# Nine neighbouring rows of w_mod on a partition, and c loaded to match

## The chip, the cores and the metric

The kernel runs on one core of one Trainium2 chip. The metric is the device time of one execution in microseconds (us); the lower the better. Engines are named as in the profile: PE is TensorE (PEld its weight loads), DVE is VectorE, ACT is ScalarE, POOL is GpSimd, SP is SyncE, which only issues DMAs here.

## What is computed

A diffusion-transformer block with adaptive layer norm, in bf16. Two samples (B = 2) of N = 256 tokens with D = 1152 features:

```python
def reference(x, c, wqkv, wo, w_mod):
    B, N, D = x.shape
    mod = (_silu(c) @ w_mod).reshape(B, 6, 1, D)
    shift_a, scale_a, gate_a, shift_m, scale_m, gate_m = [mod[:, i] for i in range(6)]
    h = _layernorm(x, axis=-1) * (1 + scale_a) + shift_a
    qkv = h @ wqkv
    q, k, v = (qkv[..., :D].copy(), qkv[..., D:2 * D].copy(), qkv[..., 2 * D:].copy())
    p = _softmax(jnp.einsum('bqd,bkd->bqk', q, k) * D ** (-0.5), axis=-1)
    a = jnp.einsum('bqk,bkd->bqd', p, v) @ wo
    return x + gate_a * a
```

`w_mod` has 1152 rows of 6 x 1152 columns; only the first three sixths of the columns (shift, scale, gate) are used. `c` has one row of 1152 features for each sample. The product `silu(c) @ w_mod` sums over the 1152 features, and the sum may be taken in any order, as long as feature i of c meets row i of w_mod.

## The kernel before

**Tiles.** A feature dimension of 1152 is cut into KT = 9 blocks of P = 128 partitions, the 512 tokens (T) into TT = 4 tiles of 128. `x_sb` holds the tokens on partitions; `xn` is x normalized; `xnT` is xn transposed (features on partitions), made by nine PE transposes into `tp` for each token tile, and copied out by ACT or DVE. `hTs` is xnT times (1 + scale); the K projection is made from hTs alone, as a shift of h adds the same to all scores of one query. `hT` has scale and shift and feeds Q and V.

**c and the modulation.** c is loaded at line 118 on ACT's DMA queue as `c_sb`, 18 partitions (sample and block) of 128 features. PE transposes it at line 157 into `cT_ps` in PSUM, so that a partition holds the features p, p + 128, p + 256 and so on of both samples. `e_sb` is exp(-c) by ACT (line 166). `silu_c` (line 170) makes the silu on DVE: add one, reciprocal, times c, into `scT_f` (128 partitions x 9 x 2); ACT then copies it, repeated 27 times along the columns, to `scT_rep` in bf16. `sc_rhs(kk)` is block kk of it, the moving operand of the modulation's matmuls.

`wmod_v` (line 49) is the view of w_mod in which partition p and block kk mean row kk * 128 + p. `load_mod` issues loads from it on SP: `wS` (scale), `wH` (shift) and `wG` (gate, in the buffer of wS). `scale_A(kk)` multiplies block kk of wS with sc_rhs(kk), four matmuls of 54 columns, into `psS0` and `psSA`; `scale_B` and `shift_block` do the same for the other columns and for the shift. The gate is made on DVE: 18 `gate_step`s multiply a block of wG by the column of scT_f for that block and add it to `gacc`, and POOL sums gacc over the partitions to `gate_bc`, whose end is multiplied into `wo_last`.

**Fillers.** Behind the transpose of c, PE runs eight matmuls of 512 columns on `ident` and `junk_rhs` into `junk_ps`; their result isn't used. `ident` is made on POOL (lines 99 and 100), `junk_rhs` on DVE (line 105).

**Order.** The wrapper `_Rec` (line 65) records every instruction of PE, DVE, ACT and SP; `pin` fixes each engine's order to the order of the program text. So most instructions have line 74, the wrapper's call, in the profile. On DVE the statistics of x tile 1 come first, then the silu of c, then the statistics of x tile 0, the normalization of tile 1 and of tile 0. On PE: the transpose of c, the fillers, one matmul each that presets psSA and psS0 with ones, scale_A(0) and (1), the transposes of tile 1, scale_A(2) and (3), the transposes of tile 0, scale_A(4) to (8), then the K projection. SP issues x tiles 1, 0 and 3, five loads of wS, then pieces of wK with x tile 2 between them, the rest of wS, wK and wH, and later wqv, wG and wO. The last wait of the start is that of `scaled(0, ...)`, the first hTs, which needs psS0 and xnT of tiles 0 and 1.

## Time and profile before

| | us |
|---|---|
| median of 3 runs | 102.11 (101.9 to 102.24) |
| the profiled execution | 101.58 |
| its span, first to last instruction | 99.6 |
| PE busy in the span | 91.3 |
| DVE, ACT, POOL busy | 67.2, 29.3, 28.5 |
| DMA | 21.04 MB, mean 211 GB/s |

The page cuts the span into 40 slices of 2.5 us; each digit is a busy share in tenths:

```profile
PE   0979899899999999999999999999999999999930
PEld 0318788874466444444458756656678656656620
DVE  1595885462165999999973999922148578798930
ACT  5057513520060872332240563221146200000000
POOL 5033312000000000000000000079999700599940
...
DMA  2999999999999999999997000000000002020321
```

PE and the DMA engines start together; the loads keep the DMA engines full until about 55 us, and PE is busy until the end. POOL's work at 65 to 79 us is the sum of the gate over the partitions, and at 86 to 96 us the product into wo_last. In a line of the timeline the columns are start, duration, engine, source line, operation, what is written from what, shapes, count, and in brackets how long the engine had idled and what ended that.

### The profile page before, as it was taken

The numbers are of one execution on the slowest core, as the hardware profiler recorded it, in microseconds if no ns is written. First come the engines' busy times: TensorE is split into PE (matmuls) and PEld (weight loads), VectorE is DVE, ScalarE is ACT, GpSimd is POOL, SyncE is SP. The second block draws the span as 40 slices with busy tenths as digits, with TensorE's granted clock in tenths as the row PEclk, the third lists the DMA queues.
The fourth block names the chain that finished last, engine by engine and source line by source line (L and its number), as shares of the span: only waits on it lengthen the run. The fifth ranks groups of instructions, "written<-read, shape, count | busy, mean of one in ns | idle before, by whom it ended". The sixth has DMA issues, their size and how long they took to land.

```text
span 99.6 us, 1801 instructions
## 1 busy us (share of the span) xinstructions
PE 91.3 (92%) x733; PEld 56.9 (57%) x733; DVE 67.2 (67%) x129; ACT 29.3 (29%) x58; POOL 28.5 (29%) x29
## 2 busy tenths in 40 slices
PE   0979899899999999999999999999999999999930
PEld 0318788874466444444458756656678656656620
DVE  1595885462165999999973999922148578798930
ACT  5057513520060872332240563221146200000000
POOL 5033312000000000000000000079999700599940
PEclk9999999999999999999999999999999999999999
DMA  2999999999999999999997000000000002020321
GB/s 61 296 284 382 400 391 389 384 405 403 381 388 390 393 405 374 372 371 375 409 408 282 22 0 0 0 0 0 0 0 10 0 0 87 31 84 34 118 79 40
DMA packets 16338, 21.04 MB, mean 211 GB/s; under 512 B 1355, under 2 KB 10827, under 8 KB 16331
## 3 DMA queue, kind: packets, MB, share of 16 engines
q1 hardware_dynamic: 16160, 20.93, 58.4%
q8 instruction: 5, 0.08, 0.3%
q10 hardware_dynamic: 171, 0.02, 0.1%
q14 instruction: 2, 0.02, 0.0%
HBM read 19.76 MB, written 1.18 MB: 210 GB/s over the span
## 4 chain that ended last, share of the span: by engine, by line
issue 51%; POOL 23%; DMA 10%; POOLq 8%; DVE 3%; SPq 1%; PE 1%; ACT 0%
POOL gate_bc L549 14%; POOL wo_last L570 9%; POOLq L649 8%; DMA x_sb<-in_x_dram 5%; DMA wK<-in_wqkv_dram 5%; DVE stats L74 1%; SPq L74 1%; PE ps L74 1%; POOL rstd L198 1%; DVE xn L74 0%; DVE hTs L74 0%; DVE mv_all L74 0%; POOL rstd L197 0%; ACT o_sb L74 0%; POOLq L570 0%
## 5 line engine op out<-in xcount | busy, mean ns | idle before, releaser
L549 POOL PARTITION_ALL_REDUCE gate_bc<-gacc x2 | 13.7, 6886 | 49.9 <-DVE gacc L74 49.9
L74 DVE SCALAR_TENSOR_TENSOR gacc<-wG,scT_f,gacc 128x1152 f32<-128x1152 bf16 x16 | 22.7, 1418 | 0.5
L74 PE MATMUL ps<-wqv,hT 128*128 128x384 bf16 x108 | 17.9, 327 | 0.0
L74 PE MATMUL ps<-hT,wqv 128*128 128x512 bf16 x81 | 17.6, 380 | 0.0
L74 PE MATMUL ps<-wO,attnT 128*128 128x384 bf16 x99 | 16.3, 327 | 0.0
L74 PEld LDWEIGHTS <-attnT 128*128 128x128 bf16 x117 | 10.9, 98 | 6.9 <-issue 0.2
L74 PEld LDWEIGHTS <-hT 128*128 128x128 bf16 x108 | 10.5, 98 | 6.7
L74 PEld LDWEIGHTS <-wK 128*128 128x128 bf16 x137 | 11.1, 97 | 5.8 <-issue 0.5
L74 PEld LDWEIGHTS <-wqv 128*128 128x128 bf16 x81 | 7.8, 97 | 9.6 <-DVE hT L74 0.4
L74 PE MATMUL acc<-hTs,wK 128*128 128x128 bf16 (+2 forms) x102 | 12.9, 279 | 0.4 <-DVE hTs L74 0.4
L570 POOL TENSOR_TENSOR wo_last<-wO,gate_bc 128x384 bf16<-128x384 bf16 x9 | 10.0, 1142 | 6.8 <-issue 6.8
L74 ACT CAST qkT<-ps 128x512 bf16<-128x512 f32 x10 | 5.8, 583 | 10.9 <-PE ps L74 10.9
L74 DVE TENSOR_TENSOR o_sb<-ga,x_sb 128x384 bf16<-128x384 f32 x11 | 7.9, 718 | 0.4
L74 DVE TENSOR_TENSOR ga<-ps,gate_bc 128x384 f32<-128x384 f32 x11 | 6.1, 554 | 2.8 <-PE ps L74 2.8
L74 ACT CAST v_sb<-ps 128x384 bf16<-128x384 f32 x10 | 4.8, 478 | 9.6 <-PE ps L74 9.6
L74 DVE BATCH_NORM_STATS2 stats<-x_sb 128x6 f32<-128x384 bf16 x9 | 4.5, 545 | 2.2 <-DMA x_sb<-in_x_dram 2.2
L74 ACT CAST o_sb<-ps 128x64 bf16<-128x64 f32 x1 | 0.2, 212 | 18.5 <-PE ps L74 18.5
L74 DVE CAST v_sb<-ps 128x384 bf16<-128x384 f32 x2 | 1.1, 557 | 6.0 <-PE ps L74 6.0
L74 DVE CAST attnT<-ps 128x512 bf16<-128x512 f32 (+1 forms) x6 | 3.5, 603 | 1.8 <-PE ps L74 1.8
L74 DVE CAST qkT<-acc 128x512 bf16<-128x512 f32 x3 | 1.9, 684 | 4.1 <-PE acc L74 4.1
L74 DVE TENSOR_SCALAR hTs<-xnT,s1p 128x256 bf16<-128x256 bf16 (+1 forms) x21 | 4.2, 270 | 0.6 <-ACT xnT L74 0.5
L74 PE MATMUL ps<-hTs,wK 128*128 128x512 bf16 x19 | 4.6, 378 | 0.0
(76 smaller groups left out, 88.2 us busy)
## 6 DMA issues: line engine op xcount, KB each, us to landing
wqv<-in_wqkv_dram SPq DMA_DIRECT2D x5, 864.0 KB, 10.7
wG<-in_w_mod_dram SPq DMA_DIRECT2D x3, 864.0 KB, 9.7
wO<-in_wo_dram SPq DMA_DIRECT2D x3, 864.0 KB, 8.6
wH<-in_w_mod_dram SPq DMA_DIRECT2D x4, 576.0 KB, 10.4
x_sb<-in_x_dram SPq DMA_DIRECT2D x4, 288.0 KB, 3.1
wS<-in_w_mod_dram SPq DMA_DIRECT2D x4, 256.0 KB, 5.6
wK<-in_wqkv_dram SPq DMA_DIRECT2D x4, 256.0 KB, 5.1
wK<-in_wqkv_dram SPq DMA_DIRECT2D x1, 864.0 KB, 11.0
```

The costliest lines, as they stand in the source:

```text
L74: r = fn(*a, **k)
L198: nc.gpsimd.tensor_tensor(out=rstd[:, t : t + 1], in0=rstd[:, t : t + 1], in1=neg_half, op=ALU.pow)
L549: ar = nc.gpsimd.partition_all_reduce(gate_bc[:, b, :], gacc[:, b, :], P, bass.bass_isa.ReduceOp.add)
L570: nc.gpsimd.tensor_tensor(out=wo_last[:, k, :], in0=wO[:, k, D - TAILW :], in1=gate_bc[:, B - 1, D - TAILW :], op=ALU.mult)
L649: with _tile.TileContext(nc) as tc:
```

## The change

Row p * 9 + kk of w_mod now goes to partition p, block kk, and c is loaded so that partition p holds features 9p to 9p + 8 of both samples. c then comes in the layout in which the silu is wanted, 128 partitions x 2 x 9, and is read from SBUF; the transpose and its PSUM tile are gone. The order of the instructions that remain is as before. The slices of columns that are loaded, and the number of loads, stay.

```diff
-    wmod_v = w_mod.rearrange("(kk p) (s n) -> p kk s n", p=P, s=6)
+    wmod_v = w_mod.rearrange("(p kk) (s n) -> p kk s n", p=P, s=6)
...
-    c_sb = const.tile([2 * KT, P], BF16)
+    c_sb = const.tile([P, B, KT], BF16)
     x_sb = act.tile([P, TT, D], BF16)
     nc.scalar.preload_act_table_set("natural_log_exp_and_others")
-    nc.scalar.dma_start(out=c_sb, in_=c.rearrange("b (k p) -> (b k) p", p=P))
+    nc.scalar.dma_start(out=c_sb, in_=c.rearrange("b (p k) -> p b k", p=P))
...
-    cT_ps = psum_b.tile([P, 2 * KT], BF16, tag="pb")
-    ten.transpose(cT_ps, c_sb, ident[: 2 * KT, : 2 * KT])
+    cT = c_sb.rearrange("p b k -> p (b k)")
     junk_ps = psum_a.tile([P, 512], F32, tag="pa")
...
     fillers(8)
     e_sb = small.tile([P, 2 * KT], F32, tag="e_sb")
-    sca.activation(out=e_sb, in_=cT_ps, func=ACT.Exp, scale=-1.0)
+    sca.activation(out=e_sb, in_=cT, func=ACT.Exp, scale=-1.0)
...
         vec.tensor_tensor(
             out=scT_f.rearrange("p k b -> p b k"),
-            in0=cT_ps.rearrange("p (b k) -> p b k", b=B),
+            in0=c_sb,
             in1=e_sb.rearrange("p (b k) -> p b k", b=B),
             op=ALU.mult,
         )
```

## The prediction

> **What bounds the kernel now.** I read the page's busy shares first, then the chain of waits from its end, then the waits, then the first 14 us in order of time, then the DMA queues of the first 4 us. PE is the engine with work nearly everywhere:

> ```profile
> PE 91.3 (92%) x733; PEld 56.9 (57%) x733; DVE 67.2 (67%) x129; ACT 29.3 (29%) x58; POOL 28.5 (29%) x29
> ```

> The end is released by a POOL chain, and that chain is released by VectorE, which has itself waited for PE. Chain of waits, then the list of waits:

> ```profile
> 65.43 13.69 POOL gate_bc L549 x2
> ...
> 86.94 8.92 POOL wo_last L570 x8
> ...
> 95.90 0.60 PE ps L74 x11
> ```

> ```profile
> POOL gate_bc L549 <- DVE gacc L74: 49.9, 1, 49.9
> ...
> DVE mx L74 <- PE s_ps L74: 2.0, 1, 2.0
> ...
> PE ps L74 <- POOL wo_last L570: 0.9, 1, 0.9
> ```

> The row maximum `mx` runs at 53.8 us and had to wait 2.0 us for the scores of PE; the gate steps, the all-reduce and `wo_last` follow it without a break. PE is busy in every microsecond from 20 to 53 (5.00 of 5.00 us in each stretch), so the scores come when the first 20 us let them. So whatever the change does to the start, late or early, moves the end by the same amount: a later start has nothing to hide in after 21 us, and an earlier one is good for up to the 2.0 us that `mx` waits. All of the change lies in the start. In order of time (start, duration, engine, work, and in brackets the idle time before it):

> ```profile
> 2.72 0.19 PE L74 MATMUL cT_ps<-ident,c_sb 18*128 18x18 bf16 x1 [2.72 <-DMA c_sb<-in_c_dram]
> 2.84 3.59 PE L74 MATMUL junk_ps<-junk_rhs,ident 128*128 128x512 bf16 x8
> ...
> 3.59 1.48 DVE L74 BATCH_NORM_STATS2 stats<-x_sb 128x6 f32<-128x384 bf16 x3 [2.21 <-DMA x_sb<-in_x_dram]
> ...
> 5.26 0.11 DVE L74 TENSOR_SCALAR e_sb<-e_sb 128x18 f32<-128x18 f32 x1
> ...
> 5.71 0.18 DVE L74 TENSOR_TENSOR scT_f<-cT_ps,e_sb 128x18 f32<-128x18 bf16 x1
> ...
> 7.46 0.23 PE L74 MATMUL psS<-scT_rep,wS 128*128 128x54 bf16 x1 [0.61 <-DMA wS<-in_w_mod_dram]
> ...
> 8.24 1.14 PE L74 MATMUL tp<-ident,xn 128*128 128x128 bf16 x9 [0.24 <-DVE xn L74]
> ...
> 9.56 1.14 PE L74 MATMUL tp<-ident,xn 128*128 128x128 bf16 x9
> ...
> 11.29 0.29 DVE L74 TENSOR_SCALAR hTs<-xnT,psS 128x256 bf16<-128x256 bf16 x1
> ```

> The path runs: first x load (lands just before 3.59), VectorE without a gap to xn(1) at 7.60 to 8.18, PE's transposes at 8.24, the two scale steps, the transposes of 9.56, the copies of xnT, hTs at 11.29, and PE's projection from 11.63 on. The PE waits at 7.46 (for wS) are not on it: PE would only wait for xn at 8.24 instead.

> **What is removed.** One weight load of 0.10 us and one matmul of 0.19 us, and with them PE's wait for c. PE idled there anyway, so by themselves they save nothing. But they stood ahead of the eight fillers. Now the fillers need only `junk_rhs` (VectorE, done at 0.90 + 0.48 = 1.38) and `ident` (POOL, 1.35 + 0.29 = 1.64). They start at about 1.70 in place of 2.84, 1.14 us sooner, and end at 5.29 in place of 6.43. The two small opening matmuls (to 6.85 now) follow, and then PE waits for wS until 7.46: some 1.75 us idle in place of 0.61. That wait costs nothing unless PE's clock minds it (below).

> **What is changed in VectorE and ScalarE.** The product `scT_f` reads c from SBUF and not from PSUM. It took 178 ns; the nearest 18-column rows that read SBUF alone are 114 ns (add) and 267 ns (reciprocal). So between -0.06 and +0.09 us, on the path, since VectorE has no gap from 3.59 to 7.55. It is nearer the 114 ns row, having no reciprocal, but has two tensor inputs: I take -0.03. The exponential (186 ns from PSUM; the 128x1 `nmean` row from SBUF 203 ns) has cover: ScalarE then waits 2.8 us.

> **What is added: c in 256 runs of 18 bytes.** Before, c came as 18 runs of 256 bytes on the ScalarE queue; now each of 128 partitions takes two runs of nine bf16, 16 runs for each of the 16 DMA engines. DMA queues of the first 4 us (packets, MB, share of 16 engines' time):

> ```profile
> q1 hardware_dynamic: 312, 0.65, 55.2%
> q10 hardware_dynamic: 27, 0.00, 0.6%
> ```

> q10 is c's queue: 0.6% of 16 x 4 us is 0.38 us, by 27 packets 14 ns each. q1 is the x loads: 55.2% is 35.3 us, by 312 packets 113 ns each. Price of c's 16 runs on each engine: from below 16 x 14 = 0.22 us, less the at most 0.04 us (two runs and an end mark) that it took before, 0.18 us; from above, if a tiny run costs as much as a row of x, 16 x 113 = 1.8 us. The nearer row in size and queue is the 14 ns, so 0.18. x goes to all 128 partitions through the same engines at the same time, eight rows on each, so at least half of c's runs go in before the first x load is done: 0.1 to 0.18 us late, and I count 0.17, a little above the middle since a run of 18 bytes may well cost somewhat over 14 ns. It is on the path (VectorE waits 2.21 us for just this load), so it counts in full: xn(1) later, transposes later, hTs later, all else as before.

> [...]

> Does c itself come late? If its runs alternate with x's, 16 x (14 + 113) = 2.0 us after x begins, that is about 4.1 in place of 2.7. The exponential (0.19) must be done by 5.26, when VectorE adds one: cover of 0.9 us is left. If it were gone, the first statistics of x(0), queued behind it on VectorE, would be late by as much.

> **w_mod's order.** The number and size of pieces stay (slices of 512, 640 or 1152 columns, one row a piece), and so do the issues and their order on SP's queue, and c's on ScalarE's; only which rows go to a partition changes. Loads of 864 KB take 9.7 us for w_mod (rows 13.8 KB apart), 10.7 for wqkv (6.9 KB) and 8.6 for wo (2.3 KB): no order by distance. Their spread, 10%, is the bound: of wS's 5.6 us to landing, 0.56 either way. Sooner saves nothing (PE then waits for xn). Later by 0.56 puts the first two scale steps at 8.02; their eight matmuls, 0.045 us apart, end the issue at 8.38, so the transposes come 0.15 us later. The wait of 0.61 is the cover, and I take 0. Sum: 0.17 - 0.03 = +0.14 us. Silu, scale, shift and gate pair the same feature of c with the same row of w_mod as before.

> The profiled execution is a span of 99.6 us and 2.0 us around it, 101.58 in all; the change makes it 101.72. The median of the runs is 0.53 above it, so 102.25.

> **Rivals.** *The clock opens later (slower).* The page's clock row reads 9 from the start, but the eight 512-column fillers take 3.59 us, 0.45 each, while later 81 of that shape take 17.64 us, 0.218 each: PE starts at half pace. In the rows the pace changes at 10.69 (four scale matmuls per 0.20 us before, per 0.10 after). Busy time of PE in four equal stretches that end there or after:

> ```profile
> 0.44:3.86 3.42, 1.14 (x4) 1.00 0.63 183
> 3.86:7.27 3.41, 2.93 (x9) 1.00 0.94 267
> 7.27:10.68 3.41, 2.98 (x38) 1.00 1.05 381
> ```

> If the change of pace needs a stretch this densely filled, the stretch to 7.27 loses over a microsecond of fillers and the one to 10.68 loses the delay of x. Then full pace comes a stretch later, say 3.2 us (7.46 to 10.69), at 13.9. The 16 scale matmuls left go at 0.05 in place of 0.025, +0.4 us; from 12.0 to 13.9 the 256-column matmuls go at 0.218 in place of 0.109 (six take 0.82), +0.95; PE's wait of 0.30 at 17.8 gives some back. About +1.05 with the 0.14 above, +1.2: 103.3. For it: the fillers are most of what PE does before 7.4. Against it: all 3.59 us of them changed nothing within 4 us here, so they may not matter at all. [...]

> *The clock opens sooner (faster).* If the pace follows the fillers' start, or the earlier fillers meet such a stretch better, PE is at full pace before 8.24. Then the first nine transposes take half, the second nine start with xn(0) (8.82 + 0.58 = 9.40) and end their first four by 9.84; the two copies (0.43 and 0.49) end at 10.83, and hTs starts at 10.88 in place of 11.29: -0.41, and wK's first piece, issued at 4.63 with 5.1 us to landing (the median of its kind), is there. 102.11 - 0.41 = 101.7; a later x load would take back 0.14.

> *Dear runs (slower).* If each 18-byte run costs like a row, the eight ahead of x's rows put the first load 8 x 113 = 0.9 us late: 103.0, at the utmost 1.8: 103.9. It decides from about 35 ns a run (8 x 35 = 0.3 us). Against it: 14 ns at 256 bytes.

> **Chances.** A measurement here tells 0.3% (0.31 us) from no change. The forecast, +0.14, own range 102.0 to 102.5: 0.40, of it 0.13 slower by more than that (c's runs at 30 ns or so) and 0.02 faster. Clock later 0.25, all slower. Dear runs 0.10, all slower. Clock sooner 0.25, 0.22 of it faster and 0.03 within. Slower 0.48, within 0.28, faster 0.24. The range runs from a little under the faster rival to the slower one, 101.6 to 103.3, and leaves out the upper end of the two slow ones and the lower end of the fast one, under 0.2.

> **What will show it.** The fillers at 1.7 and some 1.7 us of PE idle ahead of psS at 7.5; q10 with 256 more packets, less 18, of about 14 ns; the first statistics at 3.7 to 3.8 in place of 3.59; hTs as much later than 11.29; and the same distance at `mx` and at the end. A pace change far from 10.7 shows one of the clock rivals; a first x load over 0.4 us late shows dear runs; psS waiting for wS beyond 8.0 shows that w_mod's order matters. I am wrong if hTs moves without the first x load or the pace having moved.

## The result and the profile after

The changed kernel takes 103.49 us in the median (102.95 to 104.8) where the kernel before takes 102.11; the ratio is 1.0123, 95% interval 1.0082 to 1.0163. (Ratios here and below leave out the executions that ran over 1.5% above the fastest of their kernel, so a ratio need not be the quotient of two medians.) A second set of runs, with the experiments below, gave 1.0164 (1.0112 to 1.0217). So the change costs some 1.2 to 1.6%, against a forecast of +0.14 us. The time lies just above the range, which ended at 103.3.

The profiled execution took 103.77 us, with a span of 102.0 in place of 99.6. The start in order of time, the changed kernel:

```profile
1.70 3.59 PE L74 MATMUL junk_ps<-junk_rhs,ident 128*128 128x512 bf16 x8 [1.70 <-POOL ident L100]
...
3.49 1.48 DVE L74 BATCH_NORM_STATS2 stats<-x_sb 128x6 f32<-128x384 bf16 x3 [2.11 <-DMA x_sb<-in_x_dram]
3.67 0.22 ACT L74 ACTIVATE e_sb<-c_sb 128x18 f32<-128x18 bf16 x1 [1.67 <-DMA c_sb<-in_c_dram]
...
5.16 0.11 DVE L74 TENSOR_SCALAR e_sb<-e_sb 128x18 f32<-128x18 f32 x1
...
5.61 0.18 DVE L74 TENSOR_TENSOR scT_f<-c_sb,e_sb 128x18 f32<-128x18 bf16 x1
...
6.86 0.23 PE L74 MATMUL psS<-scT_rep,wS 128*128 128x54 bf16 x1 [1.16 <-DMA wS<-in_w_mod_dram]
...
8.33 0.16 DVE L74 SCALAR_TENSOR_TENSOR nb<-mv_all,rstd 128x1 f32<-128x1 f32 x1 [0.88 <-POOL rstd L197]
8.53 0.58 DVE L74 TENSOR_SCALAR xn<-x_sb,rstd,nb 128x1152 bf16<-128x1152 bf16 x1
9.16 1.14 PE L74 MATMUL tp<-ident,xn 128*128 128x128 bf16 x9 [1.76 <-DVE xn L74]
...
12.49 0.29 DVE L74 TENSOR_SCALAR hTs<-xnT,psS 128x256 bf16<-128x256 bf16 x1 [0.33 <-PE psS L74]
```

Nothing is late up to 7 us: the first statistics run at 3.49 (3.59 before), c and its exponential are there well before 5.16, and even the first wS comes sooner. Then VectorE stands for 0.88 us in front of the first `nb`, waiting for POOL, and with it xn(1) and the first transposes come 0.92 us late (9.16 against 8.24). POOL alone, in the kernel before and then in the changed one:

```profile
5.44 0.26 POOL L197 TENSOR_SCALAR rstd<-mv_all 128x1 f32<-128x1 f32 x1 [3.29 <-DVE e_sb L74]
...
5.79 0.60 POOL L198 TENSOR_TENSOR rstd<-rstd,neg_half 128x1 f32<-128x1 f32 x1
...
7.64 0.21 POOL L197 TENSOR_SCALAR rstd<-mv_all 128x1 f32<-128x1 f32 x1 [1.25 <-DVE nb L74]
```

```profile
5.34 0.26 POOL L196 TENSOR_SCALAR rstd<-mv_all 128x1 f32<-128x1 f32 x1 [3.20 <-DVE e_sb L74]
7.53 0.21 POOL L196 TENSOR_SCALAR rstd<-mv_all 128x1 f32<-128x1 f32 x1 [1.93 <-DVE mv_all L74]
7.70 1.44 POOL L197 TENSOR_TENSOR rstd<-rstd,neg_half 128x1 f32<-128x1 f32 x2
```

The two steps of rstd are an addition and a power. Before, POOL ran addition and power for tile 1, then both for tile 0. Now it runs both additions first, and the addition for tile 0 has to wait for tile 0's statistics until 7.53; the power for tile 1, ready since 5.6, stands behind it. POOL is the one engine whose order the kernel doesn't write out by hand: `pin` is called for PE, DVE, ACT and SP. The planner, given a program in which the silu takes c straight from a load, put POOL's instructions in another order. The diff shows nothing of it; a comparison of the two programs' POOL instructions does.

How the distance grows along the profiled execution (start in us):

| | before | after | distance |
|---|---|---|---|
| first nb | 7.46 | 8.33 | 0.87 |
| first transposes | 8.24 | 9.16 | 0.92 |
| first hTs | 11.29 | 12.49 | 1.20 |
| row maximum mx | 53.81 | 55.49 | 1.68 |
| sum of the gate on POOL | 65.43 | 67.11 | 1.68 |
| first wo_last | 85.87 | 88.35 | 2.48 |

From the transposes to mx it grows by 0.76. That fits PE at half pace for longer: a scale step of four matmuls takes 0.18 us up to the last one at 12.17, where the kernel before takes 0.10 from 10.69 on. The profile's record of the granted clock begins with its first change, here to full clock, at 13.83 in place of 10.68. The projection starts at 12.84, so its first 1.0 us runs at half pace and costs half of that, about the 0.48 from hTs to mx. From 67 to 88 us it grows by another 0.80, POOL's pause ahead of wo_last, 7.55 us in place of 6.75. In the profiles of the variants below that pause lies anywhere from 6.75 to 7.62 without any edit to that work (7.49 with w_mod's order alone), so I take this last step for a variation of one execution.

### The profile page after: what moved, and what is told of

It is laid out like the page before. It is cut to its first block, busy times and chain, and to the rows that moved or that the text cites. A ratio compares the mean times of both kernels' runs of the same rounds, so it can differ in the third digit from the quotient of the medians.

```text
span 102.0 us, 1800 instructions
## 1 busy us (share of the span) xinstructions
PE 92.0 (90%) x732; PEld 57.4 (56%) x732; DVE 67.9 (67%) x129; ACT 29.3 (29%) x58; POOL 28.4 (28%) x29
## 4 chain that ended last, share of the span: by engine, by line
issue 50%; POOL 24%; POOLq 8%; DVE 8%; PE 4%; DMA 3%; ACT 0%; DVEq 0%
POOL gate_bc L548 13%; POOL wo_last L569 9%; POOLq L648 8%; DVE stats L74 4%; DMA x_sb<-in_x_dram 3%; PE tp L74 2%; POOL rstd L197 1%; DVE xn L74 1%; DVE hTs L74 1%; PE psSA L74 1%; DVE mv_all L74 1%; PE ps L74 1%; POOL rstd L196 0%; PE psS L74 0%; DVE e_sb L74 0%
## 5 line engine op out<-in xcount | busy, mean ns | idle before, releaser
L74 DVE SCALAR_TENSOR_TENSOR gacc<-wG,scT_f,gacc 128x1152 f32<-128x1152 bf16 x16 | 22.7, 1418 | 0.5
L74 PE MATMUL ps<-wqv,hT 128*128 128x384 bf16 x108 | 17.9, 326 | 0.0
L74 PE MATMUL ps<-hT,wqv 128*128 128x512 bf16 x81 | 17.6, 379 | 0.0
L74 PE MATMUL ps<-wO,attnT 128*128 128x384 bf16 x99 | 16.3, 326 | 0.0
L74 PEld LDWEIGHTS <-attnT 128*128 128x128 bf16 x117 | 10.9, 98 | 7.5 <-issue 0.8
L74 PEld LDWEIGHTS <-wK 128*128 128x128 bf16 x137 | 11.3, 99 | 6.0 <-issue 0.4
L74 PEld LDWEIGHTS <-hT 128*128 128x128 bf16 x108 | 10.5, 98 | 6.7
L74 PE MATMUL acc<-hTs,wK 128*128 128x128 bf16 (+2 forms) x102 | 13.4, 285 | 0.3 <-DVE hTs L74 0.3
L74 PEld LDWEIGHTS <-wqv 128*128 128x128 bf16 x81 | 7.9, 98 | 9.6 <-DVE hT L74 0.4
L74 ACT CAST qkT<-ps 128x512 bf16<-128x512 f32 x10 | 5.8, 582 | 10.9 <-PE ps L74 10.9
L74 DVE TENSOR_TENSOR o_sb<-ga,x_sb 128x384 bf16<-128x384 f32 x11 | 8.3, 751 | 0.4
L74 DVE TENSOR_TENSOR ga<-ps,gate_bc 128x384 f32<-128x384 f32 x11 | 6.1, 555 | 3.0 <-PE ps L74 2.8
L74 ACT CAST v_sb<-ps 128x384 bf16<-128x384 f32 x10 | 4.8, 478 | 9.6 <-PE ps L74 9.6
L74 DVE BATCH_NORM_STATS2 stats<-x_sb 128x6 f32<-128x384 bf16 x9 | 4.5, 549 | 2.1 <-DMA x_sb<-in_x_dram 2.1
L74 PE MATMUL tp<-ident,xn 128*128 128x128 bf16 x36 | 3.9, 265 | 2.1 <-DVE xn L74 1.8
L74 ACT CAST o_sb<-ps 128x64 bf16<-128x64 f32 x1 | 0.2, 212 | 19.1 <-PE ps L74 19.1
L74 PE MATMUL junk_ps<-junk_rhs,ident 128*128 128x512 bf16 x8 | 3.6, 630 | 1.7 <-POOL ident L100 1.7
L74 DVE CAST v_sb<-ps 128x384 bf16<-128x384 f32 x2 | 1.1, 558 | 6.0 <-PE ps L74 6.0
L74 ACT COPY xnT<-tp 128x640 bf16<-128x640 bf16 (+1 forms) x5 | 3.2, 650 | 6.5 <-PE tp L74 6.5
L74 DVE TENSOR_SCALAR hTs<-xnT,s1p 128x256 bf16<-128x256 bf16 (+1 forms) x21 | 4.2, 272 | 1.1 <-ACT xnT L74 1.0
## 6 DMA issues: line engine op xcount, KB each, us to landing
wqv<-in_wqkv_dram SPq DMA_DIRECT2D x5, 864.0 KB, 11.5
wG<-in_w_mod_dram SPq DMA_DIRECT2D x3, 864.0 KB, 10.7
wH<-in_w_mod_dram SPq DMA_DIRECT2D x4, 576.0 KB, 10.7
```

Source lines behind the costliest of these rows:

```text
L74: r = fn(*a, **k)
```

## Experiments

"POOL held" below means that POOL's operations on rstd and nb are recorded and pinned, in the order of the program text, which is the order of the kernel before:

```diff
+    gps = _Rec(nc.gpsimd, pool_seq)
...
-        nc.gpsimd.tensor_scalar_add(out=rstd[:, t : t + 1], in0=mv_all[:, t, 1:2], scalar1=EPS)
-        nc.gpsimd.tensor_tensor(out=rstd[:, t : t + 1], in0=rstd[:, t : t + 1], in1=neg_half, op=ALU.pow)
+        gps.tensor_scalar_add(out=rstd[:, t : t + 1], in0=mv_all[:, t, 1:2], scalar1=EPS)
+        gps.tensor_tensor(out=rstd[:, t : t + 1], in0=rstd[:, t : t + 1], in1=neg_half, op=ALU.pow)
...
+    pin(pool_seq)
```

Every ratio is to the kernel before, run beside it on the same chip; the rows come from more than one chip.

| variant | POOL's order | fillers | ratio (95%) |
|---|---|---|---|
| changed kernel | new | 8, from 1.7 us | 1.0123 (1.0082 to 1.0163) |
| the same, again | new | 8, from 1.7 | 1.0164 (1.0112 to 1.0217) |
| changed, POOL held | old | 8, from 1.7 | 1.0068 (1.0025 to 1.0112) |
| the same, again | old | 8, from 1.7 | 1.0051 (0.9997 to 1.0105) |
| changed, fillers late | new | 8, from 3.4 | 1.0096 (1.0059 to 1.0134) |
| changed, POOL held, fillers late | old | 8, from 3.4 | 0.9958 (0.9910 to 1.0005) |
| changed, POOL held, 12 fillers | old | 12, from 1.7 | 0.9948 (0.9907 to 0.9989) |
| before, new POOL order | new | 8, behind c | 1.0124 (1.0089 to 1.0158) |
| before, fillers early | old | 8, from 1.7 | 1.0054 (1.0018 to 1.0091) |
| before, early, 12 fillers | old | 12, from 1.7 | 0.9959 (0.9919 to 0.9999) |
| before, 10 fillers | old | 10, behind c | 0.9958 (0.9920 to 0.9997) |
| before, w_mod's order alone | old | 8, behind c | 0.9988 (0.9953 to 1.0022) |

**The changed kernel with POOL held.**

> Theory P (POOL's order): in the changed kernel POOL computes both additions of rstd (tiles 1 and 0) before the first power, so nb(1) on VectorE waits for the second addition; 8.33 in place of 7.46 us. With POOL held to the old order, nb(1) comes at about 7.4, the first transposes at about 8.1 to 8.3 in place of 9.16, hTs at 11.2 to 11.5 in place of 12.49, and the time falls back to 101.9 to 102.5 us, within 0.4% of the kernel before. Rival C (clock, by the earlier fillers and the longer gap): the transposes come sooner too, but the pace still changes a stretch later than 10.7, and the time stays at 102.8 to 103.3 us. Rival D (c's small runs): the first x load is late and the time stays above 102.6.

102.45 us. VectorE's line, to be set beside the 8.33 above:

```profile
7.51 0.10 DVE L74 SCALAR_TENSOR_TENSOR nb<-mv_all,rstd 128x1 f32<-128x1 f32 x1
```

The wait is gone, the transposes start at 8.29. But hTs still came late, behind the scale matmuls (psS) at half pace, 0.18 us a step:

```profile
11.61 0.29 DVE L74 TENSOR_SCALAR hTs<-xnT,psS 128x256 bf16<-128x256 bf16 x1 [0.33 <-PE psS L74]
```

The time is 0.68% over the kernel before: POOL's order explains about half, and something is left. Run again:

> The changed kernel with POOL's order held, once more, on the same chip as the three others: C 102.3 to 102.8 us, 0.3 to 1.0% over the kernel before, the pace change in the trace at 10.5 to 14 us.

1.0051, with an interval that just touches one.

**The kernel before with POOL's new order.** The powers of tiles 1 and 0 are both issued after the addition for tile 0:

```diff
         gps.tensor_scalar_add(out=rstd[:, t : t + 1], in0=mv_all[:, t, 1:2], scalar1=EPS)
-        gps.tensor_tensor(out=rstd[:, t : t + 1], in0=rstd[:, t : t + 1], in1=neg_half, op=ALU.pow)
+        for u in {1: (), 0: (1, 0), 2: (2,)}[t]:
+            gps.tensor_tensor(out=rstd[:, u : u + 1], in0=rstd[:, u : u + 1], in1=neg_half, op=ALU.pow)
```

> The kernel before, with nothing changed but POOL's order: additions of rstd for tiles 1 and 0, then both powers. Theory P: nb(1) at 8.4 to 8.5 in place of 7.46, the first transposes at about 9.25 in place of 8.24, hTs 0.9 to 1.2 us later, 103.0 to 103.6 us. Rivals C and D: the fillers and c's load are as before, so the time stays at 101.9 to 102.4 us, save for at most 0.2.

103.17 us, 1.0124: POOL's order alone, with c, w_mod and the fillers untouched, costs about as much as the whole change. The same two lines in its profile:

```profile
7.77 1.44 POOL L74 TENSOR_TENSOR rstd<-rstd,neg_half 128x1 f32<-128x1 f32 x2
```

```profile
8.41 0.16 DVE L74 SCALAR_TENSOR_TENSOR nb<-mv_all,rstd 128x1 f32<-128x1 f32 x1 [0.88 <-POOL rstd L74]
```

The 0.88 us are not all of it. In this execution, the longest of the six at 104.11 us, PE stands idle for 1.35 us ahead of the transposes (0.24 before), the clock record begins only at 15.23, and mx comes at 56.20, 2.39 us later than before. So in this execution PE also stayed at half pace for longer, though nothing was done to the fillers: the stretch of 3.41 us in which PE waits for xn, from 8.40, is 2.58 us busy, where the kernel before had 2.98 from 7.27 and full pace behind it.

**w_mod's order alone.** Only line 49 is changed in the kernel before; c keeps its layout, so features of c meet other rows of w_mod: the output is another one, the work is the same.

> The kernel before with the new order of w_mod's rows alone; c is loaded and transposed as before, so features of c meet other rows of w_mod and the output is another one; the work is the same. Theory P: POOL's order is the old one here, and the time is that of the kernel before, 101.9 to 102.4 us. If w_mod's order matters to the loads: the wait for the first wS is 0.3 us or more longer or shorter and the time moves by over 0.3 us.

101.88 us, 0.9988: no cost shows. The 256 KB loads of wS take 5.5 us to landing (5.6 before), the 864 KB loads of wG 9.7 (9.7). With this, what is left of the loss must come from c's load or from the fillers.

**The kernel before with the fillers early.**

```diff
-    ten.transpose(cT_ps, c_sb, ident[: 2 * KT, : 2 * KT])
...
-    fillers(8)
+    fillers(3)
+    ten.transpose(cT_ps, c_sb, ident[: 2 * KT, : 2 * KT])
+    fillers(5)
```

> The kernel before with POOL's order held as it was, and the transpose of c put behind the third of the eight fillers, so that the fillers run from 1.7 to about 5.4 us in place of 2.84 to 6.43. c, w_mod and all loads are as before. If the earlier fillers and the longer gap after them are what is left of the loss with POOL's order held (C): the pace of PE changes later on average, hTs comes at up to 11.8, and the time is 102.5 to 102.9 us. If it is c's small runs or w_mod's order: the time stays at 101.8 to 102.3.

102.52 us, 1.0054. With c's old load, moving the same eight fillers 1.1 us ahead costs about as much as is left in the changed kernel with POOL held (1.0068 and 1.0051), and hTs is as late and waits for the same:

```profile
11.64 0.29 DVE L74 TENSOR_SCALAR hTs<-xnT,psS 128x256 bf16<-128x256 bf16 x1 [0.34 <-PE psS L74]
```

**The changed kernel with POOL held and the fillers late.**

```diff
-    vec.memset(junk_rhs, 1.0)
+    for _ in range(4):
+        vec.memset(junk_rhs, 1.0)
```

> The changed kernel with POOL's order held, and junk_rhs filled four times in place of once, so that the eight fillers start at about 2.8 us, as in the kernel before. C: the time falls from 102.5 to 101.8 to 102.3 us. If c's small runs or w_mod's order cost the rest: it stays at 102.4 to 102.9.

101.81 us, 0.9958. The fillers started later than meant, at 3.42, since each fill of junk_rhs begins 0.17 us after the end of the one before; so they end just before wS. With c's small runs and w_mod's new order in place, the loss is gone; whether there is a gain is open, as the interval reaches 1.0005. Its PE, to be set beside the 1.14 us for nine transposes:

```profile
3.42 3.57 PE L74 MATMUL junk_ps<-junk_rhs,ident 128*128 128x512 bf16 x8 [3.42 <-DVE junk_rhs L74]
...
8.37 0.68 PE L74 MATMUL tp<-ident,xn 128*128 128x128 bf16 x9 [0.74 <-DVE xn L74]
```

PE is at full pace at 8.37, and hTs comes at 10.80.

**The changed kernel with the fillers late and POOL's new order.**

> The changed kernel with POOL's order left as it is (both additions first) and junk_rhs filled four times, so that the fillers start at about 3.4 us and end near 6.9. If the two causes are separate, this keeps POOL's share alone: nb(1) at 8.3 to 8.4, the first transposes at 9.2, and 0.9 to 1.2 us more than the same kernel with POOL's order held (101.8): 102.6 to 103.0. If the whole loss were the clock's: 101.7 to 102.1.

103.28 us, 1.0096; against the same kernel with POOL held (0.9958) the order is 1.4% in the new layout, as it was 1.2% in the old. The ten executions lie between 101.58 and 104.25, so this ratio is looser than its interval says. The profiled one is the fastest of them and not typical: the other nine took 102.85 or more. In it the clock opened at 7.26 and stayed open, and PE waits for the late xn at full pace:

```profile
9.30 0.68 PE L74 MATMUL tp<-ident,xn 128*128 128x128 bf16 x9 [1.60 <-DVE xn L74]
```

VectorE still waits 0.88 us for POOL, but hTs comes at 11.36, only 0.56 us behind the variant with POOL held, and mx at 53.91, 0.59 us behind it and 0.10 us behind the kernel before. What the other nine did is not shown. So there are two causes, each of which costs by itself, but they don't simply add up: alone they give 1.0124 and 1.0054, together 1.0123 and 1.0164. In the profiles POOL's order costs more where PE is at half pace (2.39 us at mx above) than where it is not (0.59).

**The changed kernel again.**

> The changed kernel once more on the same chip as the other two: 102.9 to 103.8 us, 0.8 to 1.6% over the kernel before.

103.88 us, 1.0164. This execution shows the clock itself. Its stretches of 3.41 us, PE alone (stretch, length, PE busy and count, granted clock, DMA share, GB/s):

```profile
5.49:8.90 3.41, 0.55 (x10) 1.00 1.03 336
8.90:12.32 3.42, 3.03 (x43) 0.50 1.04 396
12.32:15.73 3.41, 3.04 (x36) 1.00 1.07 366
```

Here full pace came at 5.49, behind the early fillers (the first scale matmuls, at 6.59 and 6.71, are 0.12 us apart, against 0.19 in the profiled execution), but PE then worked only 0.55 us of the next 3.41, and behind that the granted clock was 0.50 for just the stretch in which the transposes run (9.29 to 11.5). In the profiled execution of the changed kernel the stretches lay otherwise:

```profile
3.59:7.01 3.42, 2.20 (x10) 1.00 0.94 304
7.01:10.42 3.41, 1.65 (x24) 1.00 1.05 378
10.42:13.83 3.41, 3.10 (x40) 1.00 1.06 379
```

The clock column reads 1.00 there only because the record begins at 13.83; the pace of the rows is half until then (1.14 us for nine transposes, against 0.68 with the fillers late). So in one of these two executions the early fillers were followed by half pace until 13.83, and in the other by full pace at 5.49 that was gone again at 8.90.

**Fillers without a gap.** Three variants fill PE up to the first scale matmul: the changed kernel with POOL held and `fillers(12)`, the kernel before with 3 fillers, the transpose and 9 more, and the kernel before with `fillers(10)`, all with POOL held.

> The changed kernel with POOL's order held and 12 fillers in place of 8, so that PE works without a gap from 1.7 to about 6.8 us and then takes the scale matmuls. Theory P alone: as with 8 fillers, 101.9 to 102.5 us, hTs at 11.2 to 11.5. If the pace of PE is set by how densely it worked before (C): the pace changes before 8 us, the nine transposes of a tile take about 0.7 us in place of 1.14, hTs comes at 10.8 to 11.0 and the time is 101.4 to 101.9 us.

> The kernel before with POOL's order held, c transposed behind the third filler and 12 fillers in all, from 1.7 to about 7.1 us. If the dense work from 1.7 us on is what made 12 fillers fast in the changed kernel (C), then it does as much here: 101.2 to 101.9 us, pace changed before 8 us in most executions. If the new layout itself gave that gain: 102.0 to 102.4.

> The kernel before with POOL's order held as it was and 10 fillers in place of 8, from 2.84 to 7.3 us, so that no gap is left before the scale matmuls. C: the pace changes before 8 us in most executions, 101.3 to 101.9 us. If the density before 7.4 does not matter: 102.0 to 102.3.

0.9948, 0.9959 and 0.9958. In the last, where c landed sooner and the fillers begin at 2.29 and not at 2.84, PE's fillers and transposes:

```profile
2.29 4.45 PE L74 MATMUL junk_ps<-junk_rhs,ident 128*128 128x512 bf16 x10
...
8.28 0.68 PE L74 MATMUL tp<-ident,xn 128*128 128x128 bf16 x9 [0.91 <-DVE xn L74]
```

By these ratios all three are faster than the kernel before, by a little and in either layout, so no gain of the new layout's own shows. It is a near thing: the intervals end at 0.9989, 0.9999 and 0.9997, and the median of all twelve executions of the first is 102.11 us, not the 101.4 to 101.9 expected and no less than that of the kernel before. Which is the best isn't settled. The simplest is two more fillers in the kernel before. (Holding POOL was part of each. The kernel before with that alone was not run, but its three variants keep POOL's old order, with nb at 7.50 to 7.53.)

## Why the prediction was wrong

**The step that failed: "all else as before".** It stands behind the delay of the x load, and the description of the change says likewise that the order of the remaining instructions stays. That holds for the four pinned engines. POOL's order changed, VectorE waited 0.88 us for a power that had been computable for two microseconds, and the sum lacked a term of about 1.3 us (0.0124 times 102.1, the kernel before with that one edit; 0.9 to 1.6 by the interval). The wait itself is 0.88 us. The rest fits PE's pace, as in the one profile with the clock at 15.23, but how it spreads over executions isn't shown. No case of the prediction had it. The row for it was there: rstd on POOL stands on the path between the statistics and xn, and POOL is missing from the list of pinned engines.

**The clock rival was real, and had a chance of only 0.25.** Its order of events held: the earlier fillers leave PE idle longer ahead of wS (1.41 us with POOL held and 0.91 in the kernel before with early fillers, against 0.61), and full pace comes later by less than a stretch. The clock record begins at 13.36 with POOL held and at 12.96 in the kernel before with early fillers, against 10.68. What sets the moment no run shows. For an execution in which this happens its +1.05 us was about right: mx comes at 54.81 and 54.62 in these two, 1.00 and 0.81 us later than the 53.81 before. Over all executions it is 0.5% to 0.7%, 0.5 to 0.7 us; how often it happens one profile of each kernel doesn't show. The argument against it, that the fillers "may not matter at all", was wrong: the same fillers moved cost 0.5%, and fillers up to the first scale matmul bring 0.4 to 0.5% by the ratios.

**The faster rival's price was close, its cause the other way round.** It put hTs at 10.88 and the gain at 0.41 us, if PE is at full pace before 8.24. In the four profiles with full pace ahead of the transposes and POOL held, hTs comes at 10.70 to 10.80, and the ratios put the gain at 0.4 to 0.5 us. Their intervals reach from nothing to over 0.9 us, so it is in part luck that the numbers lie so near. And it takes later or more fillers: the earlier ones alone brought full pace in one profile, at 5.49, and it was gone by 8.90.

**c's small runs: mis-sized, and below.** The DMA queues of the first 4 us in the changed kernel:

```profile
q10 hardware_dynamic: 272, 0.00, 3.8%
```

3.8% of 16 x 4 us is 2.43 us, by 272 packets (256 of 18 bytes and 16 of 4) 8.9 ns each, not 14. The first statistics are not later: they start at 3.49 to 3.73 in the seven profiles with c's new load, at 3.58 to 3.66 in the six with the old. The 0.17 us doesn't show; the rival of dear runs falls. The reason given for cover, c there by 4.1 and needed by 5.26, held: the exponential runs at 3.67.

**What held.** The fillers run from 1.70 to 5.29 as worked out. The product of the silu took 178 ns from PSUM and takes 178 from SBUF, so the -0.03 was 0. w_mod's order costs nothing that shows. The shift at the start is carried on: none of the 1.20 us at hTs is given back by mx, which is 1.68 us later.

**What stays open.** Why the planner orders POOL otherwise. It isn't the shape of c's load or the number of fillers: with c in one contiguous run a partition, with 4, 11 or 12 fillers, or with an unrelated transpose ahead of the fillers, the program has the new order; with w_mod's view alone, or with c's transpose behind three fillers, the old. It goes with where the silu gets c from. That was read from the built programs; no chip run tells more of it.

## What to carry to other kernels

An edit can reorder an engine that it doesn't touch, if that engine's order is left to a planner: compare the instruction order of every engine before and after, and pin the small ones too where they stand on the path. Here the fillers paid by where they ended, not by when they started: taking away the wait ahead of them widened the gap behind them (PE's wait for wS from 0.61 to 1.16 us). In the kernel before with the same start at 1.7 us, eight fillers gave 1.0054 and twelve 0.9959. Before an early wait is removed, ask what its end was timing.

## What the runs showed of the hardware

Busy time alone doesn't tell what follows a step. Counting back in steps of 3.41 us from where each clock record begins, the six profiles with a stretch of 3.35 to 3.41 us busy ahead of the transposes all had full pace right behind it. Of less filled stretches, 2.98 in the kernel before and 3.10 in the changed one were followed by full pace; 2.93 in the kernel before, 3.02 with w_mod's order alone and 3.23 in the kernel before with early fillers were followed by half. Half came back behind 0.55 us busy of 3.41 in the changed kernel run again, and behind 0.47 and 1.58 at the ends of the kernel before and of the changed one; behind 1.81, in the kernel with late fillers and POOL's new order, the clock stayed full. By what rule, these runs don't show.

DMA runs of 18 bytes took 8.9 ns a packet in the changed kernel, 2 GB/s by the bytes against the 20 GB/s of x's rows in the kernel before (2304 bytes in 113 ns). As time on the queue they were no dearer than the 14 ns a packet of c's old load, and nothing on the path waited for them: the exponential of c ran at 3.67 and was needed at 5.16.
